# Linear attention with a gated feed-forward: the order around batch 1's q and x, and two feed-forward groups moved to the attention's PSUM banks

## The chip, the cores and the metric

The kernel runs on one core of one Trainium2 chip. A core has five engines that work side by side and meet at semaphores: TensorE (PE in the profile, with PEld for its weight loads), VectorE (DVE), ScalarE (ACT), GpSimd (POOL) and SyncE (SP). Data reaches the core's on-chip memory by DMA. TensorE writes its results to PSUM, which has eight banks; a bank holds 512 fp32 values in each of 128 partitions. The metric is the device time of one execution in microseconds (us).

## The reference

There are eight batches, each with eight heads of 576 tokens and a head size of 64. `phi(x)` is `x + 1` for positive x and `exp(x)` otherwise, which the kernel takes as `min(exp(x), max(x, 0) + 1)`.

```python
q_p, k_p = phi(q), phi(k)
kv  = einsum('bhsd,bhse->bhde', k_p, v)
z   = sum(k_p, axis=2)
num = einsum('bhsd,bhde->bhse', q_p, kv)
den = einsum('bhsd,bhd->bhs', q_p, z)[..., None] + 1e-6
x   = (num / den) -> one row of 512 for each of the 4608 tokens
h   = x @ w_in                       # 512 -> 2048
g   = h / (1 + exp(-beta * h))
out = g @ w_out                      # 2048 -> 512
```

## The kernel before

The attention of a batch yields `x`, and the two matrix products follow, which are most of TensorE's work. A batch has 576 tokens: 512 of them go through the feed-forward as one tile of the batch (four token tiles t = 0 to 3 of 128), and the 64 odd ones (t = 4) of all eight batches are collected in `xT_tail` and go through it at the end as a ninth tile.

**H phase** (`h_phase`): 16 groups `ff` of 128 hidden units. A group is four matmuls of 512 columns (`h_mm`) into one PSUM bank, and then one SiLU on ScalarE (`silu`) that reads the bank and writes `g`. **Y phase** (`y_phase`): for each token tile 16 matmuls of 512 columns (`y_mm`, in four parts `i`, one for each quarter of `w_out`) into one bank, a copy to the on-chip buffer `y_sb` (of which there are three) on VectorE, and two output DMAs on SP (`y_out`). H0, Y0, H1, Y1 and so on follow one another. The attention of the next batches is placed between the groups by lists of side work (`at(sh, n, ...)` runs it behind group n).

**Order.** The schedule is written by hand: every engine runs its instructions in the order in which the program emits them. The tile framework adds the waits. A tile is taken from a pool with a fixed number of buffers; an instruction that writes a tile waits for whoever still reads what stood there.

**PSUM.** Four banks are the pool `mmps` (`mm_tile`), for the h groups and the y tiles in turn. Up to the end of Y0 the other four belong to `misc` and `num0` (two tiles of one bank each). From H1 on they are the pool `numps`: two tiles of two banks each (`num_tile`), for the attention.

**Y0**, the stretch that the change is about, is written out (L718 to L768), because batch 1's attention still uses plain transposes on TensorE. In its order:

- Parts i = 0 and 1 of all four y tiles (32 matmuls). Meanwhile ScalarE takes exp of batch 1's q and k, and VectorE the rest of phi (L144, L148, L155) and the scaling of `w_out`.
- `q_trans(1, (0, 1))`: eight transposes of `phi_q` into a `num0` tile, copied out by ScalarE (L243). Then part i = 2 of y tiles 0 and 1, `q_trans(1, (2, 3))`, the scaling of the last quarter of `w_out`, and part 2 of y tiles 2 and 3.
- `z_products` and `kv_direct`, `dens`, then part 3 of y tile 0, and `numer0`, whose quotient VectorE takes (L398).
- `x_trans1(0)` to `(3)`: four transposes each, copied by ScalarE into `xT` (L419); part 3 of the other y tiles stands between them. Part 3 ends y tile t, and `y_out` follows.
- ScalarE's order here is: the exps of batch 2's q (they need the DMA of `xq`), the four copies of L419, the exps of batch 2's k, a table load for SiLU, and then H1's SiLUs (L446).
- VectorE's order: four quotients, four copies of y, phi of batch 2's q, phi of batch 2's k.

**H1** needs the whole of `xT`, since each matmul covers 512 tokens. Its group ff takes the bank of y tile ff for ff = 0 to 3, and group 4 the bank that group 0's SiLU has read. Behind group 0 stand the two transposing DMAs of batch 2's `phi_q` on SP (`q_trans_dma(2)`, for `numers` at the end of H1), behind group 2 two transposes of batch 1's odd tokens (`q_odd_trans(1)`, L284) and the loads of batch 3, and behind group 8 `kv_both(2)`, which needs `phi_k` of batch 2.

The division of a batch's attention writes tiles `xs` (four buffers): t = 0 to 4 for batches 2 to 7.

Of the kernel before, what the change touches and what calls it, by code (L numbers as in the profile page):

```python
# [9 lines left out]
BF16 = mybir.dt.bfloat16  # L10
# [6 lines left out]
def kernel(  # L17
# [10 lines left out]
    nc = tc.nc  # L28

    B, H, S, D = q.shape  # L30
    DM = H * D
    DFF = moe_w_in.shape[1]
    P = 128
# [14 lines left out]
    work = ctx.enter_context(tc.tile_pool(name="work", bufs=2))  # L48
# [89 lines left out]
    st = {}  # L138
# [7 lines left out]
    def phi_relu(b, a, pr, x):  # L146
        r = work.tile([P, 2, J, D], BF16, tag="r", name="r", bufs=2)
        nc.vector.tensor_scalar(r, x, 0.0, 1.0, ALU.max, ALU.add)  # L148
        st[b, a, pr, "r"] = r
# [4 lines left out]
    def phi_min(b, a, pr, j0=0, j1=J):  # L154
        nc.vector.tensor_tensor(  # L155
            st[b, a][:, pr, j0:j1].rearrange("p j (h d) -> p j h d", h=2),
            st[b, a, pr, "e"][:, :, j0:j1].rearrange("p h j d -> p j h d"),
            st[b, a, pr, "r"][:, :, j0:j1].rearrange("p h j d -> p j h d"),
            ALU.min,
        )  # L160

    def places(b, pr):

        return slice(2 * pr, 2 * pr + 2) if b < 2 else slice(pr, 4, 2)

    def xin(b, a, pr):
        if b == 0 and a == "q":
            return q0f[:, places(b, pr)]
        return (xk if a == "k" else xq)[b % NX][:, places(b, pr)]
# [57 lines left out]
    def num_tile(name):  # L227
        return numps.tile([P, 2, 512], F32, tag="num", name=name)
# [27 lines left out]
    def q_trans(b, ts, tp, engs):  # L256

        if (b, "qT") not in st:
            st[b, "qT"] = work.tile([P, NT - 1, 2, 2, P], BF16, tag="qT", name="qT")
        slots = 1 if ts[0] == NT - 1 else 2  # L260
        tv = tp.rearrange("p (t a h i g) -> p t a h i g", a=2, h=2, i=slots, g=G)
        for k, t in enumerate(ts):
            for pr in range(2):
                for i in range(slots):
                    nc.tensor.matmul(  # L265
                        tv[:, k, pr, :, i, :], st[b, "q"][:, pr, 2 * t + i, :], identity,
                        is_transpose=True, start=True, stop=True, skip_group_check=True,
                    )
        for k, (t, eng) in enumerate(zip(ts, engs)):
            q_copy(b, k, t, tp, eng)  # L270
# [9 lines left out]
    def q_odd_trans(b, tp):  # L280

        tv = tp.rearrange("p (a n) -> p a n", a=2)
        for pr in range(2):
            nc.tensor.matmul(  # L284
                tv[:, pr], st[b, "q"][:, pr, J - 1, :], identity,
                is_transpose=True, start=True, stop=True, skip_group_check=True,
            )
        nc.scalar.copy(
            q_odd[b].rearrange("p (i a) g -> p a i g", i=2),
            tv.rearrange("p a (i g) -> p a i g", i=2),  # L290
        )
# [68 lines left out]
            scale(x, nv[:, :, n, 0:D], rden[:, :, n])  # L360

    def xs_tile(b, t):
        st[b, "xs", t] = work.tile([P, 8, D], BF16, tag="xs", name="xs", bufs=4)
        return st[b, "xs", t]

    def scale(out, num, rd):
# [42 lines left out]
    def x_trans(b, t, eng, tp):  # L409
        n = P if t < NT - 1 else G  # L410
        xv = st[b, "xs", t].rearrange("p i a d -> p (i a d)")
        tp = tp[:, 0 : KC * P].rearrange("p (c t) -> p c t", c=KC)
        for p in range(KC):
            nc.tensor.matmul(
                tp[:, p, :n], xv[:n, p * P : (p + 1) * P], identity[:n, :n],
                is_transpose=True, start=True, stop=True, skip_group_check=True,
            )
        if eng is nc.scalar:
            nc.scalar.copy(x_dst(b, t), tp[:, :, :n])  # L419
        else:  # L420
            eng.tensor_copy(x_dst(b, t), tp[:, :, :n])
# [28 lines left out]
    def mm_tile(name):  # L450
        return mmps.tile([P, 512], F32, tag="mm", name=name)

    def y_mm(b, t, i, yp, c0=0, c1=512):
        for c in range(4):
            ff = 4 * i + c
            nc.tensor.matmul(  # L456
                yp[:, c0:c1],
                g_sb[b % 2][:, ff, t * P : (t + 1) * P],
                w_out_sb[i][:, c, c0:c1],
                start=(ff == 0), stop=(ff == FC - 1), skip_group_check=True,  # L460
            )

    def rows(b, j):
        return out[b * S : (b + 1) * S, :].rearrange("(g j) m -> j g m", j=J)[j]

    def y_out(b, t, yp, c0=0, c1=512, queues=(nc.sync, nc.sync), copier=nc.vector):
        y_sb = work.tile([P, DM], F32, tag="y_sb", name="y_sb", bufs=3)
        copy(copier, y_sb[:, c0:c1], yp[:, c0:c1])
        for i in range(2):
            dst = rows(b, 2 * t + i) if b < B else rows(2 * t + i, J - 1)  # L470
            queues[i].dma_start(out=dst[:, c0:c1], in_=y_sb[i * G : (i + 1) * G, c0:c1])
# [37 lines left out]
    def misc_bf():  # L509
        return miscps.tile([P, 1024], BF16, tag="misc", name="tp")  # L510
# [18 lines left out]
    def num0_tile():  # L529
        return num0ps.tile([P, 512], F32, tag="num0", name="nps0")  # L530
# [159 lines left out]
    for ff in range(4, FC):  # L690
        hp = mm_tile("h_ps")
# [5 lines left out]
    def w_out_scale(i, n_act):  # L697
        for c in range(4):
            ff = 4 * i + c
            if c < n_act:  # L700
                nc.scalar.mul(w_out_sb[i][:, c, :], w_out_f[i][:, c, :], rbeta[:, ff : ff + 1])
            else:
                nc.vector.tensor_scalar(  # L703
                    w_out_sb[i][:, c, :], w_out_f[i][:, c, :], rbeta[:, ff : ff + 1],
                    None, ALU.mult,
                )
# [7 lines left out]
    yps = [mm_tile("y_ps") for _ in range(4)]  # L714
# [3 lines left out]
        for t in range(4):  # L718
            y_mm(0, t, i, yps[t])
    kv1 = [miscps.tile([P, 512], F32, tag="misc", name="kv1") for _ in range(2)]  # L720
    q_trans(1, (0, 1), num0_tile().bitcast(BF16), (nc.scalar, nc.scalar))
    y_mm(0, 0, 2, yps[0])
    y_mm(0, 1, 2, yps[1])
    q_trans(1, (2, 3), num0_tile().bitcast(BF16), (nc.scalar, nc.scalar))
    w_out_scale(3, 0)
    y_mm(0, 2, 2, yps[2])
    y_mm(0, 3, 2, yps[3])
    zt1 = [num0_tile() for _ in range(2)]
    for pr in range(2):
# [14 lines left out]
    for t in range(4):  # L744
        numer0(1, t, num0_tile() if t < 2 else miscps.tile([P, 512], F32, tag="misc", name="nps1"))

    def x_trans1(t):
        x_trans(1, t, nc.scalar, num0_tile().bitcast(BF16) if t < 2 else misc_bf())

    y_mm(0, 1, 3, yps[1])  # L750
    x_trans1(0)
    y_mm(0, 2, 3, yps[2], 0, 256)
    x_trans1(1)
    y_mm(0, 2, 3, yps[2], 256, 512)
    x_trans1(2)
    y_mm(0, 3, 3, yps[3], 0, 256)
    x_trans1(3)
    y_mm(0, 3, 3, yps[3], 256, 512)
    for pr in range(2):
        phi_part(2, "k", pr, xin(2, "k", pr))  # L760
    for t in range(4):
        y_out(0, t, yps[t])
    for pr in range(2):
        phi_relu(2, "q", pr, xin(2, "q", pr))
        phi_min(2, "q", pr)
    for pr in range(2):
        phi_relu(2, "k", pr, xin(2, "k", pr))
        phi_min(2, "k", pr)  # L768
    num0_pool.__exit__(None, None, None)
    misc_pool.__exit__(None, None, None)  # L770
    numps = ctx.enter_context(tc.tile_pool(name="numps", bufs=2, space=bass.MemoryType.PSUM))
# [3 lines left out]
            f()  # L775

    def h_phase(b, x, side):
        for ff in range(FC):
            hp = mm_tile("h_ps")
            h_mm(b, x, ff, hp)  # L780
            silu(b, ff, hp)
            run(side, ff)
# [18 lines left out]
    def at(side, n, *fs):  # L801
        side.setdefault(n, []).extend(fs)


    for b in range(1, B + 1):
        n = b + 1
        sh, sy = {}, {}
        if b == 1:
            at(sh, 0, lambda: q_trans_dma(2))
            at(sh, 1, lambda: [v_copy(nc.gpsimd, 2, pr) for pr in range(2)])  # L810
            at(sh, 2, lambda: q_odd_trans(1, num_tile("qop")[:, 0].bitcast(BF16)[:, 0:256]))
            at(sh, 2, lambda: load_kq(3, st[2, "qTd", "dma"]), lambda: load_v(3))
        if b == 2:
            at(sh, 8, odd_numers, odd_norms)
            at(sh, 9, lambda: [x_trans_dma(i, 4) for i in range(2)])
        if n < B:
            at(sh, 8, lambda: kv_both(n))
            at(sh, FC - 1, lambda: numers(n), lambda: [norms(n, k) for k in range(3)])
            for t in range(NT):
                at(sy, t // 3, lambda t=t: x_trans_dma(n, t))  # L820
        if n + 1 < B:
            m = n + 1
            at(sy, 3, lambda: phi_all(m, "q"))
            at(sy, 5, lambda: q_trans_dma(m), lambda: load_kq(m + 1, st[m, "qTd", "dma"]))
            at(sy, 8, lambda: phi_all(m, "k"), lambda: [v_copy(nc.gpsimd, m, pr) for pr in range(2)])
            at(sy, 9, lambda: load_v(m + 1))
        h_phase(b, xT[b % 3] if b < B else xT_tail, sh)
        y_phase(b, sy, last=(b == B))
# [30 lines left out]
```

## Time and profile before

| | us |
|---|---|
| Median of 5 runs | 287.51 |
| Lowest and highest of them | 287.05, 288.23 |
| The profiled execution | 287.68 |
| Its span, first to last instruction | 285.9 |
| TensorE busy | 275.7 (96%) |
| ScalarE busy | 161.1 (56%) |
| VectorE busy | 106.5 (37%) |
| GpSimd busy | 37.0 (13%) |

The span is what the profile's clock runs over; 1.78 us of the execution lie around it. Times in the rows count from the start of the span. A row of the timeline merges like instructions that follow each other: start, length, engine, line, operation, result and operands, how many, and in brackets the idle time before the first and what ended it. A matmul of 512 columns is shown with 0.38 us, from its start to its modelled end, but the next one starts 0.216 us after it. So TensorE is free some 0.16 us before the end that a row shows.

### The profile page before, as it was taken

How to read it: one execution, taken by the hardware profiler on the slowest of the kernel's cores; microseconds unless marked ns; L12 is line 12 of the kernel's file. 1: busy time of each engine (PE TensorE's matmuls, PEld its weight loads, DVE VectorE, ACT ScalarE, POOL GpSimd, SP SyncE). 2: the span in 40 equal slices, each digit the busy share in tenths (PEclk: the TensorE clock that was granted, in tenths of full speed). 3: DMA queues.
4: the chain of work that ended last, by engine and by line, in shares of the span. 5: the costliest groups of instructions: out<-in, count | busy, mean ns of one | idle time of the engine just before them, and what ended most of it. 6: DMA issues, size and time to landing. Idle time of an engine off the chain costs nothing.

```text
span 285.9 us, 5904 instructions
## 1 busy us (share of the span) xinstructions
PE 275.7 (96%) x2445; PEld 135.8 (48%) x2476; DVE 106.5 (37%) x255; ACT 161.1 (56%) x220; POOL 37.0 (13%) x51
## 2 busy tenths in 40 slices
PE   7799989999999999999999999999999999999994
PEld 2584447444444444444444444444444444444443
DVE  5832677625812490058104820392025100110012
ACT  5778587976556934684378526861660076018500
POOL 8732100320041000400130007000000000000000
PEclk9999999999999999999999999999999999999999
DMA  7999999699589436974896379637203410230032
GB/s 220 207 213 390 249 259 181 146 221 214 110 217 257 82 81 151 281 137 66 189 280 115 64 169 285 112 82 170 62 2 79 115 37 2 54 82 11 2 73 75
DMA packets 51723, 41.03 MB, mean 144 GB/s; under 512 B 31584, under 2 KB 43120, under 8 KB 51696
## 3 DMA queue, kind: packets, MB, share of 16 engines
q1 hardware_dynamic: 38800, 23.61, 33.7%
q0 software_dynamic: 12736, 16.91, 30.0%
q8 instruction: 19, 0.31, 0.5%
q10 hardware_dynamic: 160, 0.13, 0.2%
q14 instruction: 8, 0.07, 0.1%
HBM read 36.71 MB, written 9.44 MB: 161 GB/s over the span
## 4 chain that ended last, share of the span: by engine, by line
PE 83%; DMA 10%; ACT 3%; issue 1%; POOL 1%; DVE 0%; POOLq 0%; ACTq 0%
PE y_ps L456 41%; PE h_ps L438 38%; DMA xq<-in_q_dram 8%; DMA vf<-in_v_dram 3%; ACT e L144 2%; PE kvp L184 2%; PE nps L309 1%; PE nps_m L309 0%; ACT L144 0%; POOL xk L83 0%; PE nps L265 0%; PE nps L536 0%; ACT L446 0%; DVE phi_q L155 0%; PE kv L184 0%
## 5 line engine op out<-in xcount | busy, mean ns | idle before, releaser
L446 ACT ACTIVATE g<-h_ps,beta_c 128x512 bf16<-128x512 f32 x144 | 97.9, 689 | 93.1 <-PE h_ps L438 92.7
L456 PE MATMUL y_ps<-w_out,g 128*128 128x512 bf16 (+3 forms) x583 | 126.0, 370 | 0.9
L438 PE MATMUL h_ps<-xT,w_in 128*128 128x512 bf16 x487 | 109.3, 379 | 1.2 <-ACT g L446 0.4
L456 PEld LDWEIGHTS <-g 128*128 128x128 bf16 x600 | 57.6, 98 | 64.0
L438 PEld LDWEIGHTS <-w_in 128*128 128x128 bf16 x560 | 54.2, 98 | 65.2 <-issue 1.3
L245 DVE COPY y_sb<-y_ps 128x512 f32<-128x512 f32 (+2 forms) x37 | 24.7, 673 | 73.7 <-PE y_ps L456 68.4
L83 POOL DMA_DIRECT2D xq<-in_q_dram x7 | 5.2, 744 | 106.7 <-ACT g L446 95.7
L144 ACT ACTIVATE e<-xk 128x1152 bf16<-128x1152 bf16 x16 | 17.8, 1152 | 0.6 <-DMA xk<-in_k_dram 0.6
L144 ACT ACTIVATE e<-xq 128x1152 bf16<-128x1152 bf16 x14 | 15.5, 1155 | 0.4 <-DMA xq<-in_q_dram 0.3
L376 DVE TENSOR_SCALAR den<-nps 128x12 f32<-128x12 f32 x12 | 2.0, 164 | 35.6 <-PE nps L309 35.6
L239 DVE CAST kvd<-kvp 128x260 bf16<-128x260 f32 x6 | 2.6, 427 | 32.2 <-PE kvp L184 32.2
L438 PE MATMUL h_ps<-xT_tail,w_in 128*128 128x512 bf16 x62 | 13.9, 379 | 0.1
L367 DVE TENSOR_TENSOR xs<-nps,rden 128x512 bf16<-128x512 f32 (+1 forms) x24 | 12.2, 552 | 1.5 <-DMA xT_tail<-xs 1.2
L155 DVE TENSOR_TENSOR phi_q<-e,r 128x1152 bf16<-128x1152 bf16 (+2 forms) x17 | 11.7, 718 | 2.7 <-ACT e L144 2.4
L155 DVE TENSOR_TENSOR phi_k<-e,r 128x1152 bf16<-128x1152 bf16 x16 | 11.6, 753 | 0.3
L173 POOL CAST vaug<-vf 128x1152 bf16<-128x1152 f32 x10 | 11.2, 1160 | 1.5 <-DMA vf<-in_v_dram 1.5
L144 ACT ACT_TABLE_LOAD x6 | 7.7, 1283 | 5.5 <-DMA xq<-in_q_dram 5.4
L133 PE MATMUL warm_ps<-xT 128*128 128x512 bf16 x20 | 6.9, 497 | 1.8 <-DVE xT L96 1.5
L367 DVE TENSOR_TENSOR xs<-nps_m,rden 128x256 bf16<-128x256 f32 (+1 forms) x24 | 7.1, 350 | 4.0 <-DMA xT<-xs 3.5
L446 ACT ACT_TABLE_LOAD x6 | 7.7, 1283 | 0.1
L83 POOL DMA_DIRECT2D xk<-in_k_dram x9 | 6.8, 752 | 4.7 <-DMA g<-in_moe_w_out_dram 2.1
L703 DVE TENSOR_SCALAR w_out<-g,rbeta 128x512 bf16<-128x512 f32 x8 | 3.8, 536 | 9.0 <-DMA g<-in_moe_w_out_dram 9.0
(94 smaller groups left out, 121.0 us busy)
## 6 DMA issues: line engine op xcount, KB each, us to landing
out_dram<-y_sb SPq DMA_DIRECT2D x70, 128.0 KB, 2.4
vf<-in_v_dram SPq DMA_DIRECT2D x5, 1152.0 KB, 6.5
xq<-in_q_dram POOLq DMA_DIRECT2D x7, 576.0 KB, 10.2
xk<-in_k_dram POOLq DMA_DIRECT2D x7, 576.0 KB, 12.4
w_in<-in_moe_w_in_dram POOLq DMA_DIRECT2D x4, 512.0 KB, 12.4
g<-in_moe_w_out_dram POOLq DMA_DIRECT2D x2, 1024.0 KB, 17.4
stage<-in_moe_w_out_dram POOLq DMA_DIRECT2D x2, 1024.0 KB, 20.8
stage<-in_q_dram SPq DMA_DIRECT2D x2, 576.0 KB, 4.1
```

The costliest lines, as they stand in the source:

```text
L83: return eng.dma_start(out=dst[:, h0 : h0 + n].rearrange("p h j d -> p h (j d)"), in_=rows.rearrange("(i p) e -> p i e", p=P)[:, h0 : h0 + n],
L133: nc.tensor.matmul(warm_ps[:, 0:cols], warm[:, 0:P], warm[:, 0:cols], start=True, stop=True)
L144: nc.scalar.activation(st[b, a, pr, "e"][:, :, j0:j1], x[:, :, j0:j1], ACTF.Exp)
L155: nc.vector.tensor_tensor(st[b, a][:, pr, j0:j1].rearrange("p j (h d) -> p j h d", h=2), st[b, a, pr, "e"][:, :, j0:j1].rearrange("p h j d ...
L173: eng.tensor_copy(vaug[b % 2][:, pr, :, :, 0:D], src[:, places(b, pr)].rearrange("p h j d -> p j h d"))
L184: nc.tensor.matmul(dst[hh][c], st[b, "k"][r, pr, j, c], mov(r, j, h), start=(j == 0), stop=(j == J - 1), skip_group_check=True,)
L245: eng.tensor_copy(dst, src)
L367: nc.vector.tensor_mul(out, num, rd[..., None].to_broadcast(list(num.shape)))
L438: nc.tensor.matmul(hp[:, c0:c1], w_in_sb[ff // 4][:, kc, (ff % 4) * P : (ff % 4 + 1) * P], x[:, kc, c0:c1], start=(kc == 0), stop=(kc == K ...
L446: nc.scalar.activation(g_sb[b % 2][:, ff, :], hp, ACTF.Silu, scale=beta_c[:, ff : ff + 1])
L456: nc.tensor.matmul(yp[:, c0:c1], g_sb[b % 2][:, ff, t * P : (t + 1) * P], w_out_sb[i][:, c, c0:c1], start=(ff == 0), stop=(ff == FC - 1), ...
L703: nc.vector.tensor_scalar(w_out_sb[i][:, c, :], w_out_f[i][:, c, :], rbeta[:, ff : ff + 1], None, ALU.mult,)
```

## The change

Five things are moved.

1. In Y0, part 2 of y tiles 0 and 1 comes ahead of `q_trans(1, (0, 1))`, and the second `q_trans` stands between part 2 of y tiles 2 and 3. The call that scales the last quarter of `w_out` is emitted ahead of all that; VectorE's order stays the same.
2. Part 3 of y tiles 1 and 2 is cut in halves with the four `x_trans1` between them, and part 3 of y tile 3 is whole and last. `x_trans1(3)` is copied by VectorE, not by ScalarE.
3. VectorE takes batch 2's phi of k ahead of that of q, with the relu half of k ahead of the fourth copy of y.
4. H1's groups 3 and 4 go into the two halves (one bank each) of one `num_tile`, and `q_odd_trans(1)` moves from behind group 2 to behind group 6.
5. The odd tokens' quotient of batches 2 to 7 gets a buffer of its own, `xs_odd`.

```diff
     def xs_tile(b, t):
-        st[b, "xs", t] = work.tile([P, 8, D], BF16, tag="xs", name="xs", bufs=4)
+        if t == 4 and b > 1:
+            st[b, "xs", t] = work.tile([P, 4, D], BF16, tag="xs_odd", name="xs_odd", bufs=1)
+        else:
+            st[b, "xs", t] = work.tile([P, 8, D], BF16, tag="xs", name="xs", bufs=4)
         return st[b, "xs", t]
...
-    q_trans(1, (0, 1), num0_tile().bitcast(BF16), (nc.scalar, nc.scalar))
+    w_out_scale(3, 0)
     y_mm(0, 0, 2, yps[0])
     y_mm(0, 1, 2, yps[1])
+    q_trans(1, (0, 1), num0_tile().bitcast(BF16), (nc.scalar, nc.scalar))
+    y_mm(0, 2, 2, yps[2])
     q_trans(1, (2, 3), num0_tile().bitcast(BF16), (nc.scalar, nc.scalar))
-    w_out_scale(3, 0)
-    y_mm(0, 2, 2, yps[2])
     y_mm(0, 3, 2, yps[3])
...
-    def x_trans1(t):
-        x_trans(1, t, nc.scalar, num0_tile().bitcast(BF16) if t < 2 else misc_bf())
-
-    y_mm(0, 1, 3, yps[1])
-    x_trans1(0)
-    y_mm(0, 2, 3, yps[2], 0, 256)
-    x_trans1(1)
-    y_mm(0, 2, 3, yps[2], 256, 512)
-    x_trans1(2)
-    y_mm(0, 3, 3, yps[3], 0, 256)
-    x_trans1(3)
-    y_mm(0, 3, 3, yps[3], 256, 512)
+    def x_trans1(t, eng=nc.scalar):
+        x_trans(1, t, eng, num0_tile().bitcast(BF16) if t < 2 else misc_bf())
+
+    for t in (1, 2):
+        for i in range(2):
+            y_mm(0, t, 3, yps[t], 256 * i, 256 * (i + 1))
+            x = 2 * (t - 1) + i
+            x_trans1(x, nc.scalar if x < 3 else nc.vector)
+    y_mm(0, 3, 3, yps[3])
     for pr in range(2):
         phi_part(2, "k", pr, xin(2, "k", pr))
-    for t in range(4):
+    for t in range(3):
         y_out(0, t, yps[t])
+    for pr in range(2):
+        phi_relu(2, "k", pr, xin(2, "k", pr))
+    y_out(0, 3, yps[3])
+    for pr in range(2):
+        phi_min(2, "k", pr)
     for pr in range(2):
         phi_relu(2, "q", pr, xin(2, "q", pr))
         phi_min(2, "q", pr)
-    for pr in range(2):
-        phi_relu(2, "k", pr, xin(2, "k", pr))
-        phi_min(2, "k", pr)
...
     def h_phase(b, x, side):
+        two = None
         for ff in range(FC):
-            hp = mm_tile("h_ps")
+
+            if b == 1 and ff in (3, 4):
+                two = num_tile("h_ps2") if ff == 3 else two
+                hp = two[:, ff - 3]
+            else:
+                hp = mm_tile("h_ps")
...
-            at(sh, 2, lambda: q_odd_trans(1, num_tile("qop")[:, 0].bitcast(BF16)[:, 0:256]))
+            at(sh, 6, lambda: q_odd_trans(1, num_tile("qop")[:, 0].bitcast(BF16)[:, 0:256]))
```

## The prediction

> **What bounds the kernel now.** The page comes first: TensorE's row and the slices say that it is full nearly everywhere, at full clock.
>
> ```profile
> PE 275.7 (96%) x2445; PEld 135.8 (48%) x2476; DVE 106.5 (37%) x255; ACT 161.1 (56%) x220; POOL 37.0 (13%) x51
> ...
> PE   7799989999999999999999999999999999999994
> ...
> PEclk9999999999999999999999999999999999999999
> ```
>
> So an edit pays only where TensorE waits. The timeline of TensorE over Y0 and H1 shows where:
>
> ```profile
> 29.95 7.07 PE L456 MATMUL y_ps<-w_out,g 128*128 128x512 bf16 x31
> 37.30 0.28 PE L265 MATMUL nps<-identity,phi_q 128*128 128x128 bf16 x2 [0.28 <-DVE phi_q L155]
> 38.35 0.51 PE L265 MATMUL nps<-identity,phi_q 128*128 128x128 bf16 x6 [0.77 <-DVE phi_q L155]
> ...
> 50.04 2.75 PE L438 MATMUL h_ps<-xT,w_in 128*128 128x512 bf16 x11 [0.24 <-ACT xT L419]
> 52.63 0.27 PE L284 MATMUL qop<-identity,phi_q 128*128 128x128 bf16 x2
> 52.74 1.03 PE L438 MATMUL h_ps<-xT,w_in 128*128 128x512 bf16 x4
> 54.16 4.48 PE L438 MATMUL h_ps<-xT,w_in 128*128 128x512 bf16 x20 [0.39 <-ACT g L446]
> ```
>
> There are four stalls. With 0.16 us of modelled tail added to each bracket they are 0.44, 0.93, 0.40 and 0.55 us: 2.3 us in all, the most that any reordering here can win. Behind 54.16 no row of TensorE up to the end has a bracket; whatever this instant moves by, the end moves by.
>
> What sets 54.16? ScalarE's timeline, read backwards from there:
>
> ```profile
> 39.51 1.05 ACT L243 COPY qT<-nps 128x512 bf16<-128x512 bf16 x2
> 41.07 1.07 ACT L243 COPY qT<-nps 128x512 bf16<-128x512 bf16 x2 [0.50 <-PE nps L265]
> 44.15 0.54 ACT L658 CAST kv<-kv 64x128 bf16<-64x128 f32 x2 [2.00 <-PE kv L184]
> 45.03 2.22 ACT L144 ACTIVATE e<-xq 128x1152 bf16<-128x1152 bf16 x2 [0.34 <-DMA xq<-in_q_dram]
> 47.43 1.25 ACT L419 COPY xT<-nps 128x512 bf16<-128x512 bf16 x2 [0.18 <-PE nps L414]
> 48.75 1.25 ACT L419 COPY xT<-tp 128x512 bf16<-128x512 bf16 x2
> 49.89 2.22 ACT L144 ACTIVATE e<-xk 128x1152 bf16<-128x1152 bf16 x2
> 52.12 1.28 ACT L446 ACT_TABLE_LOAD   x1
> 53.42 1.84 ACT L446 ACTIVATE g<-h_ps,beta_c 128x512 bf16<-128x512 f32 x3
> ```
>
> The reader is to see one chain without a hole: the DMA of batch 2's q lands (45.03), two exps, four copies of xT, two exps of k, the table load, the first SiLU (53.42, 0.69 long). Group 4 starts 0.05 us after that SiLU, in whose bank it writes. The chain starts at a DMA that the change does not touch.
>
> **Y0's order (parts 1 and 2), on TensorE.** Its 32 matmuls end at 36.86 (29.95 + 32 x 0.216). Eight more of y follow, to 38.6, by when phi_q is there (38.29 by VectorE's rows): the first two stalls, 1.37 us, go. Eight transposes of 0.058 each, four of y, eight transposes, four of y bring TensorE to 41.3. There z_products needs both num0 tiles, so ScalarE's last copy of qT. The first two copies stay at 39.51, behind the exps of k; the other two follow at once, end at 41.7, and z starts at 41.74 instead of 42.69. So 0.4 of the 1.37 comes back as a wait on ScalarE, and what follows is 0.95 earlier: x_trans1(0) at 45.6, its quotient at 45.4, y's last matmul ends at 48.7 (before: 49.64). The VectorE scaling of w_out keeps its place and ends at 42.0, ahead of z's evacuation at 42.4, so it costs nothing.
>
> **The same on ScalarE.** It is through with kv at 43.7 and then waits for the DMA until 45.03, as before. Copies follow exps with a start 0.10 before the last exp's end (row 39.51 against 37.41 + 2.20), so the first xT copy starts at 47.15; TensorE delivered its tile at 46.0. Three copies at the pitch of the qT copies (0.48; in the trace of before they came at 0.66, TensorE's pace) end at 48.67. The fourth, on VectorE, starts when TensorE has transposed it (48.0) and ends at 48.4 (a qT copy of this size on VectorE took 0.41). VectorE's copy of y tile 0 moves behind it, 48.35 to 49.03 (0.68 each). H1's group 0 needs that bank: it starts at 49.1, 0.95 earlier. Batch 2's exps of k then start at 48.57 (before 49.89); their DMA was issued at 25.97 and took 21.8 to 22.1, so it has landed by 48.1.
>
> **H1's groups 3 and 4 (part 4).** Here the gain is lost. The diff reads as if five groups could now run without a SiLU. In the program as built the first matmul of group 4 still waits for ScalarE, and by the count that it waits for, no longer for group 0's SiLU but for group 3's: the framework takes the two halves as one tile, and group 3's SiLU reads it. TensorE ends group 3 at 52.5 (49.1 + 4 x 0.863). SiLU 0 starts as far behind the exps of k as before (53.42 - 49.89 = 3.53), at 52.10; three pitches of 0.575 (1.84 for three less 0.69, over two) put SiLU 3 at 53.82, its end at 54.51 and group 4 at 54.56. That is 0.40 later than now, with a new stall of 2.0 us ahead of it. q_odd_trans's 0.11 (52.63 to 52.74), hidden under the old stall, now lies behind group 6 on the full path. Sum: +0.40 + 0.11 = **+0.51 us**. On the chain: -1.32 by copies earlier, closer and fewer, +1.72 by three SiLUs.
>
> Behind this wait stand the rest of H1 and, on ScalarE, nothing that is late: group 5 needs y tile 3's copy, which waits for an output DMA as before (51.99, now some 52.4, end 53.1) and has 2 us left. Groups 6 to 8 find SiLUs 0 to 2 done.
>
> **Part 3 (k ahead of q).** kv_both(2) gets phi_k at 54.4 instead of 58.33 by VectorE's rows; TensorE asks at 59.0, so nothing is won. phi_q is ready at 56.9 instead of 55.86: y 3's copy to 53.1, two minima of k (1.42), relu and minimum of q twice (2.4). The two transposing DMAs on SP then stand 1.0 later, and land at 63.5 (the loads held by them started at 62.54 in the trace); numers asks at 66.0. Batch 3's loads on POOL and the exps in Y1 follow 1 us later: exps and table load end at 76.4 instead of 75.4, H2's first SiLU is due at 81.6. If this cover were gone it would cost 1 us at most.
>
> **Part 5.** VectorE loses its 2.5 us wait for an xT DMA at 72.48. TensorE's rows there have no bracket, so it pays nothing; of added waits there are none near, since a buffer is taken again one batch (29 us) later.
>
> **Sum.** The profiled execution goes from 287.68 to 288.19. It lies 0.17 above the median of 287.51, so on the median: **288.0**, slower by 0.18%. A measurement of this kernel can tell about 0.2% (0.57 us) from no change, so this stands just inside that.
>
> **Unknowns.** First, where the DMA of q lands. If later by d, the old chain has 0.28 to spare (47.43 against 47.15) and the new has none: up to +0.79. If earlier, the old chain does not gain (TensorE paced its copies) but the new one does, until x_trans binds it: with q 1.3 earlier copies run at 46.1, 46.7, 47.4, and k's DMA then holds it to 48.1 (sum 0.0) or comes earlier too (-0.2). Ends: -0.2 and +0.8; I take +0.51, the landing in the row. Second, the pitch of copies, 0.48 to 0.66: three copies, 0 to +0.5. I take the low end, the row of copies that did not wait for TensorE.
>
> **The clock.** After the warm-up the longest idle of TensorE before is 0.93 us, and the profile grants 1.00 there. The new stall is 2.0 us, for which no row exists. The nearest row of a slow TensorE is the start: 15 matmuls from 1.46 to 6.65, 0.346 each instead of 0.216, 1.95 us lost. So its price lies between 0 and 1.95; I take 0, nearer to the 0.93 that cost nothing.
>
> The Trainium skill ("TensorE: Matmul & The Clock Gate", Part 1: The HAM clock gate) says that the array falls back to half rate after at least one idle window of about 3.4 us. By it 2.0 us would not do, and the sum would stay at +0.51; a reading by which any longer hole starts the warm-up anew would make it +2.46. No run here shows which.
>
> **Rivals.**
> 1. *Not slower: the halves do not hold each other up.* Were the wait met earlier, group 4 would start at 52.5, group 5 find y 3's copy at 53.1 and group 6 SiLU 0 at 52.8. H1 would be through 1.5 us earlier (0.95 + 0.55): 286.0. For it speaks that the halves are different banks; against it the wait in the program. It decides as soon as group 4 can start 0.5 us sooner than 54.56. Chance 0.05.
> 2. *Not slower: q lands early.* The new chain gains up to 0.7 and ends between -0.2 and 0.0: 287.3 to 287.5. It decides from a landing 0.5 earlier. The row's own wait of 0.34 speaks for landing as the bound; five runs spread over 1.2 us say that it can move. Chance 0.15.
> 3. *Slower: the clock falls in the 2.0 us stall.* +0.51 + 1.95 = 2.46: 290.0. Chance 0.06.
> 4. *Slower: later landing or slower copies.* Each end of the unknowns alone gives +0.8 (0.51 + 0.28) or +1.0 (0.51 + 0.5), both +1.3: 288.3 to 288.8. Chance 0.22.
>
> **The numbers.** The forecast has the rest, 0.52, at 288.0, its own spread 287.7 to 288.3, a little over half of it under 288.08. Faster (under 286.94): rival 1 and a little of 2, 0.06. Slower (over 288.08): rivals 3 and 4 and 0.2 of the forecast, 0.48. Same: 0.46. The range 287.2 to 288.9 goes from the low end of rival 2 to the high end of rival 4 (with 0.1 for the measurement) and leaves out rivals 1 and 3, with 0.11.
>
> **What would show it.** No bracket at 37 and 38 on TensorE; a small wait of z on ScalarE near 41.7; H1 from 49.1; a row of group 4 near 54.6 with about 1.9 us behind "ACT g"; the transposes of L284 behind group 6; numers near 66.0; granted clock 1.00. Wrong it would be with group 4 straight behind group 3, a clock under 1 near 55, or xq landing elsewhere than 45.0.

## The result and the profile after

The changed kernel is **slower: 288.56 us** at the median of 44 executions (287.92 to 290.58) against 287.52 of 84 of the kernel before, +1.04 us; ratio 1.004, 95% interval 1.0032 to 1.0048. Forecast were 288.0 with a range of 287.2 to 288.9: the sign and the cause hold, the size fell 0.56 us short. The profiled execution took 288.27, with a span of 286.5 (before 287.68 and 285.9): in the profiled pair the difference is 0.59, and 288.19 had been forecast for it.

The page's first two parts, after (busy times and slices of the span):

```profile
span 286.5 us, 5908 instructions
...
PE 275.1 (96%) x2445; PEld 135.5 (47%) x2476; DVE 107.5 (38%) x256; ACT 160.8 (56%) x219; POOL 37.3 (13%) x51
...
PE   7799999799999999999999999999999999999994
...
PEclk9999999999999999999999999999999999999999
```

TensorE has the same work and the same share; the slice that begins at 50 us has fallen from a 9 to a 7, and the one at 36 us has risen from an 8 to a 9. The timeline of TensorE, after, from Y0 to numers:

```profile
30.42 8.80 PE L459 MATMUL y_ps<-w_out,g 128*128 128x512 bf16 x39
39.05 0.61 PE L265 MATMUL nps<-identity,phi_q 128*128 128x128 bf16 x8
...
42.13 0.58 PE L194 MATMUL nps<-ones,phi_k 64*128 64x1 bf16 x35 [0.19 <-ACT qT L243]
...
49.49 3.63 PE L441 MATMUL h_ps<-xT,w_in 128*128 128x512 bf16 x16 [0.25 <-DVE y_sb L245]
54.78 2.75 PE L441 MATMUL h_ps<-xT,w_in 128*128 128x512 bf16 x12 [1.67 <-ACT g L449]
57.37 0.28 PE L284 MATMUL qop<-identity,phi_q 128*128 128x128 bf16 x2
57.48 1.89 PE L441 MATMUL h_ps<-xT,w_in 128*128 128x512 bf16 x8
...
66.19 0.58 PE L309 MATMUL nps<-kvd,qTd 64*64 64x65 bf16 x48
```

The two stalls at 37 and 38 are gone, H1 starts 0.55 earlier (49.49 against 50.04), and then TensorE stands after 16 matmuls, that is after group 3, until 54.78. The bracket of 1.67 with the modelled tail is 1.83 of idle time. Before, group 4 started at 54.16 and numers at 65.45. ScalarE's timeline, after, has the reason:

```profile
45.09 2.22 ACT L144 ACTIVATE e<-xq 128x1152 bf16<-128x1152 bf16 x2 [0.98 <-DMA xq<-in_q_dram]
47.33 1.07 ACT L422 COPY xT<-nps 128x512 bf16<-128x512 bf16 x2
48.29 0.60 ACT L422 COPY xT<-tp 128x512 bf16<-128x512 bf16 x1
48.76 2.24 ACT L144 ACTIVATE e<-xk 128x1152 bf16<-128x1152 bf16 x2
51.02 1.28 ACT L449 ACT_TABLE_LOAD   x1
52.31 2.42 ACT L449 ACTIVATE g<-h_ps,beta_c 128x512 bf16<-128x512 f32 x4
55.85 0.69 ACT L449 ACTIVATE g<-h_ps,beta_c 128x512 bf16<-128x512 f32 x1 [1.11 <-PE h_ps L441]
```

The chain from q's landing is the one that the prediction drew, with four SiLUs in the place of one ahead of the release. The fourth ends at 54.73, group 4 starts at 54.78, and the fifth SiLU has to wait for group 4.

### The profile page after: what moved, and what is told of

It reads as the page before. It is cut to its first block, busy times and chain, and to the rows that moved or that the text cites. A ratio compares the mean times of both kernels' runs of the same rounds, so it can differ in the third digit from the quotient of the medians.

```text
span 286.5 us, 5908 instructions
## 1 busy us (share of the span) xinstructions
PE 275.1 (96%) x2445; PEld 135.5 (47%) x2476; DVE 107.5 (38%) x256; ACT 160.8 (56%) x219; POOL 37.3 (13%) x51
## 4 chain that ended last, share of the span: by engine, by line
PE 91%; DMA 3%; POOL 1%; ACT 1%; issue 1%; DVE 0%; POOLq 0%
PE y_ps L459 43%; PE h_ps L441 42%; DMA w_in<-in_moe_w_in_dram 3%; PE kvp L184 1%; PE h_ps L641 1%; PE nps L309 1%; ACT g L449 1%; POOL vf L83 1%; PE nps_m L309 0%; POOL xk L83 0%; ACT qT L243 0%; DVE y_sb L245 0%; PE nps L539 0%; PE nps L265 0%; PE tp L631 0%
## 5 line engine op out<-in xcount | busy, mean ns | idle before, releaser
L148 DVE TENSOR_SCALAR r<-xk 128x1152 bf16<-128x1152 bf16 x16 | 7.7, 516 | 0.0
```

## The experiments

Three theories stood against each other. **W**: the framework waits on the two halves of `h_ps2` as on one tile, and this is the loss. The rival: the loss comes from Y0's order or phi's. **C**: the stall is long enough for the clock of TensorE to fall in some executions.

**Separate tiles for groups 3 and 4.** The edit, against the changed kernel:

```diff
             if b == 1 and ff in (3, 4):
-                two = num_tile("h_ps2") if ff == 3 else two
-                hp = two[:, ff - 3]
+                hp = num_tile("h_ps2")[:, 0]
```

> The changed kernel, but H1's groups 3 and 4 take one num_tile each (the first half of it) instead of the two halves of one. Theory W (the whole tile is one unit for the waits): group 4 starts straight behind group 3, 0.86 us after it, and H1's stall of 2.05 us is gone; from the changed kernel's rows numers moves from 66.19 to 66.19 - 1.84 = 64.3, which is 1.1 ahead of the 65.45 of the kernel before: about 286.4 us, faster by 0.4%. Rival (the loss lies elsewhere, in Y0's order or in the phi of k): no change, 288.4. Theory C (the clock falls in the long stall in some executions, which then take 290): no execution of this kernel near 290 or at its own median plus 1.5, and none with a mean granted clock under 0.996.

286.54 us (286.17 to 289.29, 12 executions), ratio to the kernel before 0.9966, interval 0.9937 to 0.9995. TensorE's timeline:

```profile
49.43 6.22 PE L441 MATMUL h_ps<-xT,w_in 128*128 128x512 bf16 x28 [0.25 <-DVE y_sb L245]
...
64.30 0.58 PE L309 MATMUL nps<-kvd,qTd 64*64 64x65 bf16 x48
```

Twenty-eight matmuls, groups 0 to 6, without a hole; numers at the forecast 64.30. The start of H1 is the same as in the changed kernel (49.43 and 49.49), so the 1.9 us between the two (66.19 and 64.30) come from this one wait. Theory W is shown: the diff is this one line, and the wait is gone with it. On C the expectation missed: one of the 12 executions, at 289.29, had a mean clock of 0.988, although the profiled execution of this kernel has no long hole in H1.

**The changed kernel without part 4.** Groups 3 and 4 are back in `mmps`, `q_odd_trans(1)` behind group 2:

```diff
-            if b == 1 and ff in (3, 4):
-                two = num_tile("h_ps2") if ff == 3 else two
-                hp = two[:, ff - 3]
-            else:
-                hp = mm_tile("h_ps")
+            hp = mm_tile("h_ps")
...
-            at(sh, 6, lambda: q_odd_trans(1, num_tile("qop")[:, 0].bitcast(BF16)[:, 0:256]))
+            at(sh, 2, lambda: q_odd_trans(1, num_tile("qop")[:, 0].bitcast(BF16)[:, 0:256]))
```

> The changed kernel without part 4: groups 3 and 4 in mmps banks and q_odd_trans(1) behind group 2, the rest as changed. In the built program group 3 then waits for group 0's SiLU (its end in the changed kernel's rows: 53.00), so group 3 at 53.05, group 4 at 53.92 instead of 54.16, q_odd_trans hidden under the stall: numers at 65.2, 0.24 ahead of the kernel before, about 287.3 us. Theory W says that part 4 as a whole costs about 1.0 us (66.19 - 65.2) in executions at full clock. Rival: Y0's reordering brings its whole 0.95 to the end, 286.6; or it is the reordering that costs, 288.4.

287.50 us, ratio 0.9995, interval 0.9982 to 1.0008: no difference from the kernel before that could be told. The rows:

```profile
49.10 2.76 PE L441 MATMUL h_ps<-xT,w_in 128*128 128x512 bf16 x12 [0.25 <-DVE y_sb L245]
...
53.05 5.34 PE L441 MATMUL h_ps<-xT,w_in 128*128 128x512 bf16 x24 [1.08 <-ACT g L449]
```

Group 3 at 53.05 and numers at 65.20, both as expected. H1 starts 0.94 earlier but the first SiLU, on which group 3 now waits, lets numers come only 0.25 earlier (65.20 against 65.45). So part 4 alone turns the change from no difference to a loss of 1.1 us (288.56 - 287.50), and parts 1, 2, 3 and 5 together do not cost.

**Part 4 alone, in the kernel before.** The lines of part 4, and nothing else:

```diff
+            if b == 1 and ff in (3, 4):
+                two = num_tile("h_ps2") if ff == 3 else two
+                hp = two[:, ff - 3]
+            else:
+                hp = mm_tile("h_ps")
...
-            at(sh, 2, lambda: q_odd_trans(1, num_tile("qop")[:, 0].bitcast(BF16)[:, 0:256]))
+            at(sh, 6, lambda: q_odd_trans(1, num_tile("qop")[:, 0].bitcast(BF16)[:, 0:256]))
```

> The kernel before with part 4 alone: groups 3 and 4 in the halves of one num_tile, q_odd_trans(1) behind group 6. Theory W: SiLU 3 ends at 53.42 + 2.42 = 55.84, group 4 at 55.89 instead of 54.16, and 0.11 for the transposes: 287.5 + 1.84 = 289.4 in executions at full clock. TensorE is then idle from 53.5 for 2.4 us; theory C: executions with a fallen clock at about 291.1. Rival (the halves do not hold each other up): the old stall of 0.55 goes, 287.1.

289.33 us (6 executions), ratio 1.007, interval 1.0043 to 1.0098: +1.7 against the 287.62 of the kernel before that ran beside it, where W has +1.84.

```profile
55.69 2.75 PE L438 MATMUL h_ps<-xT,w_in 128*128 128x512 bf16 x12 [2.24 <-ACT g L446]
```

Numers comes at 67.09. The rival, which has a gain here, is out.

**Part 1 alone, in the kernel before.** Y's part 2 ahead of q's transposes:

```diff
-    q_trans(1, (0, 1), num0_tile().bitcast(BF16), (nc.scalar, nc.scalar))
+    w_out_scale(3, 0)
     y_mm(0, 0, 2, yps[0])
     y_mm(0, 1, 2, yps[1])
+    q_trans(1, (0, 1), num0_tile().bitcast(BF16), (nc.scalar, nc.scalar))
+    y_mm(0, 2, 2, yps[2])
     q_trans(1, (2, 3), num0_tile().bitcast(BF16), (nc.scalar, nc.scalar))
-    w_out_scale(3, 0)
-    y_mm(0, 2, 2, yps[2])
     y_mm(0, 3, 2, yps[3])
```

> The kernel before with part 1 alone (y's part 2 ahead of q's transposes). x_trans1 is 0.95 earlier; ScalarE, from q's landing on, has the four copies of xT behind the exps without a hole: from 47.3 at a pitch of 0.48 instead of from 47.43 at 0.66. The exps of k start at 49.2, SiLU 0 at 52.8, group 4 at 53.5 instead of 54.16; numers at 64.8: about 286.9 us, faster by 0.2%. Rival (the landing of q holds all of it back): no change, 287.5.

287.16 us, ratio 0.9988, interval 0.9969 to 1.0007: not to be told from no change. In the profiled execution numers did come at 64.94 (expected 64.8), 0.51 earlier than before. But its span is 285.9 like that of the kernel before (it took 287.67, 0.51 above the median of this kernel), and TensorE's timeline says where the half microsecond went in it:

```profile
65.68 7.08 PE L456 MATMUL y_ps<-w_out,g 128*128 128x512 bf16 x32
73.22 1.04 PE L456 MATMUL y_ps<-w_out,g 128*128 128x512 bf16 x4 [0.47 <-DVE xs L367]
```

In Y1, y tile 2 takes the bank that the odd tokens' quotient still reads, and VectorE stands there for a buffer of xs. This led to the next run.

**Separate tiles, with part 5 undone.** The odd tokens' quotient takes one of the four `xs` buffers again:

```diff
-        if t == 4 and b > 1:
-            st[b, "xs", t] = work.tile([P, 4, D], BF16, tag="xs_odd", name="xs_odd", bufs=1)
-        else:
-            st[b, "xs", t] = work.tile([P, 8, D], BF16, tag="xs", name="xs", bufs=4)
+        st[b, "xs", t] = work.tile([P, 8, D], BF16, tag="xs", name="xs", bufs=4)
```

> Separate tiles for groups 3 and 4, with part 5 undone (the odd tokens' quotient takes one of the four xs buffers again). With part 1 alone a new wait had come up in Y1: y tile 2 on VectorE's quotient, which waits for the DMA that reads its buffer (0.47 us at 73.22). Theory: H1 ends 1.2 us earlier here, the DMAs on SP do not, so y tile 2 waits for the quotient by about 0.9 to 1.4 us: 287.4 to 287.9, so part 5, worth nothing in the kernel before (0.2 us of room), is worth about 1 here. Rival (a part that costs and brings nothing): 286.5.

287.96 us against 286.54 with the buffer: 1.4 us in the medians, at the upper end of the 0.9 to 1.4 expected (1.7 if each is taken against the kernel before that ran beside it, 287.38 and 287.62), and slower than the kernel before (1.0031, interval 1.0009 to 1.0053). VectorE's timeline in the kernel before:

```profile
72.48 0.49 DVE L367 TENSOR_TENSOR xs<-nps_m,rden 128x128 bf16<-128x128 f32 x2 [2.51 <-DMA xT<-xs]
```

And in this kernel, with TensorE's behind it:

```profile
73.33 0.49 DVE L367 TENSOR_TENSOR xs<-nps_m,rden 128x128 bf16<-128x128 f32 x2 [4.58 <-DMA xT<-xs]
```

```profile
73.68 7.08 PE L456 MATMUL y_ps<-w_out,g 128*128 128x512 bf16 x32 [1.64 <-DVE xs L367]
```

VectorE waits 4.58 us for the transposing DMA that reads the buffer, instead of 2.51 in the kernel before. In both kernels where y tile 2 waited, it started 0.35 us behind the start of the quotient (73.68 behind 73.33, and 73.22 behind 72.87). In the kernel before this would be 72.83, and y tile 2 was due at 73.10 (behind 32 matmuls from 66.18 on): some 0.3 us of room, which an earlier H1 uses up. So part 5 is worth 1.4 us where H1 ends early. By the rows it is worth nothing in the kernel before or in the changed one; no run has it alone there.

**Separate tiles, with part 3 undone.** Phi of q ahead of phi of k, all four copies of y first:

```diff
-    for t in range(3):
+    for t in range(4):
         y_out(0, t, yps[t])
-    for pr in range(2):
-        phi_relu(2, "k", pr, xin(2, "k", pr))
-    y_out(0, 3, yps[3])
-    for pr in range(2):
-        phi_min(2, "k", pr)
     for pr in range(2):
         phi_relu(2, "q", pr, xin(2, "q", pr))
         phi_min(2, "q", pr)
+    for pr in range(2):
+        phi_relu(2, "k", pr, xin(2, "k", pr))
+        phi_min(2, "k", pr)
```

> Separate tiles for groups 3 and 4, with part 3 undone (phi of q ahead of phi of k, all four copies of y first). kv_both(2) asks at 57.42; phi of k's second half is ready at 58.7 by VectorE's rows (y 3's copy to 53.2, 3.2 for q, 2.4 for k), 1.0 later than its matmuls can use it. Theory: part 3, which is worth nothing in the changed kernel, is worth about 1 us as soon as the stall ahead of group 4 is gone: 287.5 instead of 286.5, and a wait of TensorE in kvp on phi_k. Rival (phi_k is early enough): 286.5.

286.48 us, ratio 0.9966 (0.9952 to 0.998): the same as with part 3, so the expected 1.0 us is not there. The wait on phi_k exists, at 57.79, with a bracket of 0.24. Phi_k was ready at 57.73, not at 58.7. One relu that took 1.16 us in the kernel before, beside GpSimd's copies, took 0.45 here, when the copies were all but over, and the fourth y copy was done at 52.80, 0.4 before my figure.

**Filling the stall.** Eight matmuls that nobody reads, between groups 3 and 4 of the changed kernel:

```diff
             h_mm(b, x, ff, hp)
+            if b == 1 and ff == 3:
+                dummy = num_tile("dummy")[:, 0]
+                for _ in range(8):
+                    nc.tensor.matmul(
+                        dummy, w_in_sb[0][:, 0, 0:P], x[:, 0, :], start=True, stop=True
+                    )
             silu(b, ff, hp)
```

> The changed kernel with eight matmuls of 512 columns, whose result nobody reads, between the groups 3 and 4 of H1. They take 8 x 0.216 = 1.73 us of a hole of 1.84, so the path is the same and TensorE is busy in it. Theory C (clock): the executions near 290.0 (11 of the 44 of the changed kernel, with mean granted clocks of 0.992 to 0.994) are gone, and the median falls to 288.3 or 288.4. Rival D (the long executions come from DMAs that land late): as many of them stay, at 290.

> The changed kernel with the eight unread matmuls in the hole once more, for the count of low clocks: theory C: at most as many as in the kernel before (some 1 in 8), 288.4; rival: a quarter.

288.42 and 288.29 us, 12 executions each, as expected; group 4 at 54.85 in the first profiled execution, so the path is the same. One of each twelve had a clock of 0.994 (291.14 and 290.86). That makes 2 of 24, against 11 of 44 in the changed kernel (288.65 to 290.58) and 9 of the 77 of the kernel before that ran beside these experiments. Chance alone can make such a difference in counts as small as these, so they settle neither theory C nor rival D.

The execution of 290.86 is the profiled one of the second run, and its trace shows where its time went. An answer by stretch of time gives the stretch, its length, the busy time of PE, PEld, DVE, ACT and POOL with counts, the granted clock, the DMA share and GB/s:

```profile
10.00:20.00 10.00, 7.99 (x172) 6.37 (x169) 5.26 (x17) 4.99 (x15) 3.74 (x5) 0.83 1.24 207
```

In batch 0's attention TensorE stood until 16.18 for a DMA of `w_in`, with a bracket of 1.64 (before: 0.23, until 14.37). The granted clock was 0.50 from 15.8 to 19.0, and 1.00 at 50 to 70 us. H1 began at 52.20 instead of 49.07, and its group 4 had no bracket. So in this one a late DMA and a fallen clock came together, long ahead of the place of the hole.

**A longer stall.** The last exp of k is done again, once or twice, into the same tile:

```diff
     for pr in range(2):
         phi_part(2, "k", pr, xin(2, "k", pr))
+    for _ in range(2):
+        nc.scalar.activation(st[2, "k", 1, "e"], xin(2, "k", 1), ACTF.Exp)
```

> The changed kernel with the last exp of batch 2's k done three times (two more exps on ScalarE ahead of the table load, into the same tile). SiLU 3 comes 2 x 1.07 = 2.14 us later, TensorE stands still for 4.0 us instead of 1.84 ahead of group 4, and nothing else is late: 288.4 + 2.1 = 290.5 in executions at full clock. Theory C (a longer hole lowers the clock more often, at 1.5 to 1.9 us each): mean granted clock of 0.994 or less in half of the executions or more, and those at 292 to 292.5. Rival (the low clocks have nothing to do with the hole): a sixth of them, as in the kernel before.

> The same with 18 matmuls of 512 columns (3.89 us), whose result nobody reads, in the hole. The path is the same: 290.5. Theory C: a clock of 0.994 or less no more often than in the kernel before, and no cluster at 292. Rival: as many as without the filling.

With two exps more: 292.41 us, all four executions with a clock of 0.988 to 0.993. With the hole filled by 18 matmuls: 290.75, the clock 0.997 to 1.000. TensorE's timelines, the empty hole first and then the filled one:

```profile
57.23 4.44 PE L441 MATMUL h_ps<-xT,w_in 128*128 128x512 bf16 x12 [4.53 <-ACT g L449]
```

```profile
53.00 4.05 PE L794 MATMUL dummy<-xT,w_in 128*128 128x512 bf16 x18
57.46 2.75 PE L441 MATMUL h_ps<-xT,w_in 128*128 128x512 bf16 x12 [0.41 <-ACT g L449]
```

The same twelve matmuls take 4.44 us behind the empty hole and 2.75 behind the filled one. The granted clock by stretch of time, empty and then filled:

```profile
57.00:61.00 4.00, 3.77 (x10) 1.40 (x10) 0.00 (x0) 1.41 (x3) 0.00 (x0) 0.58 0.53 134
```

```profile
57.00:61.00 4.00, 3.59 (x19) 1.67 (x18) 0.10 (x1) 2.54 (x5) 0.00 (x0) 1.00 0.44 111
```

So a hole of 4.7 us (the bracket and the tail; 4.0 had been expected) costs 1.7 us of clock on top. Theory C is shown for this length.

> The changed kernel with one more exp on ScalarE ahead of the table load: TensorE's hole is 2.9 us. At full clock 288.4 + 1.07 = 289.5. Theory C: clocks of 0.994 or less in a share between those of the changed kernel (11 of 44 at a hole of 1.84) and of the hole of 4.0 (4 of 4), so half of the executions or more, at 291.1. Rival (a threshold between 2.9 and 4.0): as often as in the changed kernel.

With one exp more: 291.0 us over 6 executions, 289.38 to 292.38, four of them with a clock of 0.987 to 0.993. The count is as C expects, but the profiled execution, one of the low ones, says something else about its own:

```profile
12.00:16.00 4.00, 3.75 (x71) 2.66 (x71) 2.08 (x8) 2.24 (x8) 1.75 (x3) 0.54 1.24 208
16.00:20.00 4.00, 4.00 (x48) 4.00 (x46) 1.77 (x6) 1.45 (x5) 0.75 (x1) 0.60 1.24 206
54.00:58.00 4.00, 1.69 (x9) 0.70 (x8) 2.92 (x5) 3.84 (x6) 0.00 (x0) 1.00 0.89 204
58.00:62.00 4.00, 4.00 (x21) 1.87 (x21) 1.36 (x3) 2.64 (x5) 0.00 (x0) 1.00 0.27 67
```

Its clock was low from 12 to 20 us, in batch 0's attention, and full behind the hole of 2.5 us. So a low mean does not tell where the clock fell, here as in the execution of 290.86 above. Whether it ever falls in the changed kernel's own hole of 1.83 us stays open: its profiled execution was at full clock, and there is no trace of a low one.

**The version that beats both.** Separate tiles, and VectorE copies y tile 0 ahead of the fourth copy of xT, since H1's group 0 waits for that bank:

```diff
+    y_out(0, 0, yps[0])
     for t in (1, 2):
         for i in range(2):
             y_mm(0, t, 3, yps[t], 256 * i, 256 * (i + 1))
...
-    for t in range(3):
+    for t in (1, 2):
         y_out(0, t, yps[t])
```

> Separate tiles for groups 3 and 4, and VectorE copies y tile 0 ahead of the fourth x_trans1 copy. H1's group 0 waited for y 0's copy (49.43 in the rows of the separate tiles); it is then due with ScalarE's third copy and TensorE's own end, near 49.0: 0.35 to 0.45 earlier, 286.1 us. Rival: the start of H1 is held by the landing of q and moves less than 0.1, 286.5.

286.00 us (285.83 to 286.38, 6 executions), ratio 0.9944, interval 0.9928 to 0.9961.

```profile
48.87 6.20 PE L441 MATMUL h_ps<-xT,w_in 128*128 128x512 bf16 x28 [0.19 <-ACT xT L422]
...
63.72 0.58 PE L309 MATMUL nps<-kvd,qTd 64*64 64x65 bf16 x48
```

H1 starts at 48.87 and is now released by ScalarE's copies; numers is 1.73 earlier than in the kernel before.

## Why the prediction was right, and by how much not

- **The step that decided, H1's groups 3 and 4, was right.** The diff alone suggested two more free banks; the program's wait of group 4 on SiLU 3 said otherwise, and it held (54.73 and 54.78). "That is 0.40 later than now" was 0.62, and "Sum: +0.51" is +0.74 at numers (66.19 - 65.45). q_odd_trans's 0.11 was exact (57.37 to 57.48). That the profiled execution then came within 0.08 of its forecast (288.27 for 288.19) is in part luck: from numers to the end it took 220.29 us, the kernel before 220.44, which hides 0.15 of the 0.74.
- **The term of the sum that was mis-sized** is "Copies follow exps with a start 0.10 before the last exp's end", "so the first xT copy starts at 47.15". It started at 47.33, 0.03 behind that end (47.30), and in the nine other traces in which nothing else held that copy back it starts 0.02 to 0.03 behind too. Of the 0.22 that group 4 came later than forecast (54.78 for 54.56), 0.12 is this, 0.06 is q's landing (45.09 for 45.03), and the rest the table and the SiLUs. The pitch of the copies was right: exps of k 1.43 behind the first copy, forecast 1.42.
- **Between the profiled pair and the medians** another 0.45 lies (1.04 against 0.59). The profiled execution of before was 0.16 above its median, that of after 0.29 below. Executions with a clock of 0.994 or less are in it: without them the medians are 288.38 (33 executions) and 287.52 (68 of the 77), +0.86. So the low clocks, which the prediction took at nothing, are worth some 0.2 of the difference of the medians; that they come from the hole is not shown. The remaining 0.12 over numers' shift of 0.74 I can't assign.
- **Y0's order.** Both stalls went, and the wait of z on ScalarE came, as said (forecast 41.74; its first matmul at 41.77, the next at 42.13 behind the copy). H1 came at 49.49 instead of 49.1: in this execution Y0 itself began 0.47 later (30.42), which q's landing covered for ScalarE but not for VectorE's copy; in four of the other traces it came at 49.07 to 49.10. It had no weight, since the chain through ScalarE sets group 4.
- **Part 3** was priced at nothing, rightly by the rows of the changed kernel (phi_k ready at 54.59, kv_both without a bracket at 59.30), though no run leaves it out there, and it brings nothing with separate tiles either. phi_q came at 56.91 (56.9).
- **Part 5** was priced at nothing, and by the rows that holds for the kernel before and for the changed one. What the prediction didn't see is how thin its cover is: some 0.3 us.
- **Rival 1** was wrong on the condition and near in the price: 286.0 forecast if the halves did not hold each other up, 286.54 with tiles that don't. H1's later start (49.43) is 0.33 of the difference.
- **Rivals 2 to 4.** q landed at 44.83 to 45.37 in the twelve traces that show it with ScalarE already waiting (before 45.03, after 45.09), never the 0.5 earlier that rival 2 needs, so rival 2 was given too much. Rival 3's mechanism is real for a hole of 4.7 us, at 1.7 us and not 1.95; for this hole it is not shown. The result lies in the middle of rival 4's range, but not for its reasons: the pitch of the copies was as forecast, and the landing 0.06 later.

## What to carry to other kernels

Before trusting a diff that seems to free a buffer, look in the built program for what the next writer waits on: two banks taken as one tile were waited for as one, and this cost 1.9 us, while two tiles cost nothing. An earlier start pays only up to the next release (here the first SiLU, a fixed distance behind a DMA's landing), and it uses up room elsewhere; a part that is worth nothing in one order (the odd tokens' buffer) can be worth 1.4 us in another. Price every part beside the others that are meant to go with it.

## What was not expected of the hardware

- A stall of TensorE of 4.7 us was followed by some 3.4 us at half clock in the profile (0.58 from 57 to 61, so 0.42 x 4 us was lost), 1.7 us in all; with unread matmuls in the hole there was none. The Trainium skill ("TensorE: Matmul & The Clock Gate", Part 1: The HAM clock gate) puts the fall behind an idle window of about 3.4 us. The 4.7 us with a fall and the profiled 2.5 us without one agree with that; the two falls of the next point, behind shorter idle times, do not, and there the traces decide.
- Most of the kernels showed a low clock in some executions, the kernel before in 9 of 77. Three such executions were profiled. In one the clock fell behind the hole of 4.7 us. In another it fell at 12 to 20 us (0.54 and 0.60), in batch 0's attention, where TensorE had not stood for longer than a bracket of 0.83 from 6 us on. In the third it fell at 15.8 to 19.0 (0.50), during a wait with a bracket of 1.64. The three falls come to some 3.4, 6.9 and 3.4 us at half clock by these shares. What sets off the last two is not shown.
- A relu of 128x1152 on VectorE took 1.16 us in the kernel before and 1.40 in the changed one while GpSimd copied (51.22 to 53.45, and 50.71 to 53.30). With separate tiles it took 0.45, although 0.39 of that lay beside the same copies, so GpSimd's copying alone does not explain the difference.
